# Moving key copies and block-mean writes of an attention + gated-FFN kernel from VectorE to ScalarE

## The chip, the cores and the metric

The kernel runs on one core of one Trainium2 chip. Its time is the device time of one launch in microseconds (us). Below, PE is TensorE, DVE is VectorE, ACT is ScalarE, POOL is GpSimd and SP is SyncE, as the profile names them. A median is given over several runs. A ratio is the mean time of one kernel's fast runs over the mean time of the other's fast runs of the same rounds, so it is not quite the ratio of the medians beside it; its 95% interval stands in brackets.

## The reference, cut to what matters

Sparse attention (a band of 16 tokens plus one key and one value for each block of 32 tokens), and then a gated feed-forward network (FFN) with a residual.

```python
k_sum = k.reshape(B, H, nb, block, D).max(axis=3)     # block keys: a maximum
v_sum = v.reshape(B, H, nb, block, D).mean(axis=3)    # block values: a mean
... softmax over the band |i-j| < 16 and over the blocks ...
return np.matmul(a, np.concatenate([v, v_sum], axis=2))
# then, with x the attention's output:
ffn_out = gelu(x @ w_gate) * (x @ w_val) @ w_out
return x + sigmoid(x @ w_res) * ffn_out
```

## The kernel before

The work is cut into eight units u of 384 tokens; units 2b and 2b+1 are batch b. While the FFN of unit u runs on PE, the operands of later attention steps are prepared on the other engines. An FFN step `fo` is a group of four matmuls into g, a group of four into vv, a Gelu of g on ACT, and a product on DVE:

```python
def fo_end(gvT, fo, g, vv):
    ge = work.tile([128, TU], F32, tag="ge", name="ge")
    nc.scalar.activation(ge[:], g[:, 0:TU], AF.Gelu)           # ACT, L404
    nc.vector.tensor_mul(gvT[:, fo, :], ge[:], vv[:, 0:TU])    # DVE, L405
```

g and vv take turns in a pool of four PSUM banks. In the FFN of units 3 and 5 DVE also prepares the keys and values of batches 2 and 3:

```python
def k_rest(kw):                       # L206
    ... nc.vector.tensor_max(km, ...)                           # L209
    nc.vector.tensor_reduce(out=ks, in_=km, op=ALU.max)         # L211: block keys
    nc.vector.tensor_copy(kw[:, 1:NT, 0:WIN], kw[:, 0:NT - 1, OWN + QT - WIN:OWN + QT])      # L213
    nc.vector.tensor_copy(kw[:, 0:NT - 1, POST:POST + WIN], kw[:, 1:NT, OWN:OWN + WIN])      # L214
    nc.vector.tensor_copy(kw[:, :, BLK0:BLK0 + NB], ks broadcast)                            # L215

def turn_sums():                      # a transpose on SP's DMA queue
    nc.sync.dma_start_transpose(out=vsB, in_=vsT)               # L271

def vsum_bc(b, hp, lo, hi):           # block means into vext, from vsB
    ... nc.vector.tensor_scalar_mul(dst, vsB broadcast, 1.0 / BLK)                           # L303

# in the loop over fo, units 3 and 5 (nb is the batch being prepared):
fo_step(st, gvT, fo)                                            # g, vv, Gelu, product
if fo in (1, 3):        v_spread(b, 0, HT // 2, fo // 2)        # DVE copies in vext, L291 and L294
if 5 <= fo < 9:         vsum_bc(b, fo - 5, 0, HT)
if fo == 0:             turn_sums(); turn_batch(nb, NP - 1, NP)
if fo in (0, 2, 4, 11): k_rest(kW[nb % 2][...])
```

The softmax here doesn't subtract the row's maximum and nothing guards it: scores larger than these inputs give would overflow.

## Time and profile before

| | before |
|---|---|
| time, median of 3 runs | 259.73 us (259.49 to 260.19) |
| span of the profiled run | 257.9 us |
| busy: PE / DVE / ACT / POOL | 97% / 69% / 50% / 39% |
| one FFN step on PE (two groups of 0.65 us) | 1.30 us |
| PE time lost in the FFN of unit 3 / unit 5 | 0.97 / 0.23 us |

The rows to look at are those of the instructions that will move. From the groups by line, each shape apart, of the kernel before (columns: line, engine, operation, tiles, shapes, count, busy us, mean ns of one, idle us before them):

```profile
L303 DVE TENSOR_SCALAR vext<-vsB 32x768 bf16<-32x768 bf16 x16 | 6.1, 380 | 0.5
L213 DVE COPY kW<-kW 128x176 bf16<-128x176 bf16 x12 | 3.7, 310 | 0.0
L214 DVE COPY kW<-kW 128x176 bf16<-128x176 bf16 x12 | 3.3, 279 | 0.0
```

The mean of L213 is 310 ns, although its shortest instance takes 198 ns: some instances took much longer, up to 0.59 us in unit 3. Of the L303 writes (median 360 ns) only the first of unit 3 was long, 0.66 us. Of these rows 8 of 16 and 8 of 12 will move.

### The profile page before, as it was taken

How to read it: one execution, taken by the hardware profiler on the slowest of the kernel's cores; microseconds unless marked ns; L12 is line 12 of the kernel's file. 1: busy time of each engine (PE TensorE's matmuls, PEld its weight loads, DVE VectorE, ACT ScalarE, POOL GpSimd, SP SyncE). 2: the span in 40 equal slices, each digit the busy share in tenths (PEclk: the TensorE clock that was granted, in tenths of full speed). 3: DMA queues.
4: the chain of work that ended last, by engine and by line, in shares of the span. 5: the costliest groups of instructions: out<-in, count | busy, mean ns of one | idle time of the engine just before them, and what ended most of it. 6: DMA issues, size and time to landing. Idle time of an engine off the chain costs nothing.

```text
span 257.9 us, 5755 instructions
## 1 busy us (share of the span) xinstructions
PE 250.2 (97%) x2249; PEld 139.5 (54%) x2249; DVE 178.3 (69%) x426; ACT 129.5 (50%) x223; POOL 101.0 (39%) x139
## 2 busy tenths in 40 slices
PE   7989999999999999999999999999999999999993
PEld 3546555566545555555554565555554665556543
DVE  5756866595598878679959768679768853764333
ACT  4855369455635637553373537453473537443310
POOL 7995542795699910996650100020001000010000
PEclk9999999999999999999999999999999999999999
DMA  7999999999999999999994995165003200130012
GB/s 157 151 151 193 199 202 199 142 209 123 151 152 165 179 129 167 125 186 202 154 134 90 146 145 103 31 153 68 1 3 86 84 0 0 33 137 3 1 41 83
DMA packets 117899, 30.16 MB, mean 117 GB/s; under 512 B 104816, under 2 KB 115504, under 8 KB 117872
## 3 DMA queue, kind: packets, MB, share of 16 engines
q0 software_dynamic: 86640, 19.11, 86.7%
q1 hardware_dynamic: 31232, 10.69, 25.6%
q8 instruction: 17, 0.28, 0.5%
q14 instruction: 10, 0.08, 0.1%
HBM read 32.51 MB, written 6.29 MB: 150 GB/s over the span
## 4 chain that ended last, share of the span: by engine, by line
PE 79%; DVE 7%; DMA 5%; POOL 4%; issue 2%; ACT 1%; POOLq 0%; DVEq 0%
PE f L432 22%; PE vv L398 19%; PE g L398 18%; PE r L416 8%; PE ao L362 3%; DMA k_sb<-in_k_dram 3%; PE gv L548 3%; DMA vext<-in_v_dram 2%; PE s L330 2%; DVE gvT L405 2%; PE xp L381 1%; POOL k_sb L175 1%; POOL vext L100 1%; DVE ks L211 1%; DVE vext L294 1%
## 5 line engine op out<-in xcount | busy, mean ns | idle before, releaser
L398 PE MATMUL vv<-xT,w_val 128*128 128x384 bf16 x364 | 74.5, 326 | 0.1
L404 ACT ACTIVATE ge<-g 128x384 f32<-128x384 f32 x87 | 42.7, 491 | 63.3 <-PE g L398 37.0
L398 PE MATMUL g<-xT,w_gate 128*128 128x384 bf16 x348 | 71.3, 326 | 0.4 <-DVE gvT L405 0.2
L405 DVE TENSOR_TENSOR gvT<-ge,vv 128x384 bf16<-128x384 f32 x91 | 50.0, 553 | 27.5 <-PE vv L398 25.5
L432 PE MATMUL f<-w_out,gvT 128*128 128x512 bf16 (+2 forms) x312 | 68.4, 363 | 0.0
L398 PEld LDWEIGHTS <-w_val 128*128 128x128 bf16 x368 | 36.0, 98 | 24.0 <-issue 0.4
L398 PEld LDWEIGHTS <-w_gate 128*128 128x128 bf16 x352 | 34.1, 98 | 23.2 <-issue 1.1
L432 PEld LDWEIGHTS <-gvT 128*128 128x128 bf16 x312 | 28.3, 98 | 28.2
L443 POOL DMA_DIRECT2D out_dram<-o x12 | 6.5, 544 | 90.9 <-DVE rz L370 76.0
L422 ACT ACTIVATE th<-r 128x512 f32<-128x512 f32 x24 | 14.2, 602 | 24.8 <-PE r L416 24.8
L437 DVE SCALAR_TENSOR_TENSOR th<-th,f 128x512 f32<-128x512 f32 (+2 forms) x26 | 16.7, 642 | 12.3 <-PE f L432 8.5
L175 POOL DMA_DIRECT2D k_sb<-in_k_dram x24 | 19.8, 839 | 12.5 <-DMA w_out<-in_moe_w_out_dram 5.2
L416 PE MATMUL r<-w_res,xT 128*128 128x512 bf16 x96 | 24.4, 380 | 0.0
L100 POOL DMA_DIRECT2D vext<-in_v_dram x28 | 23.2, 875 | 1.5 <-PE g L398 1.2
L175 POOL DMA_DIRECT2D q_sb<-in_q_dram x24 | 20.0, 875 | 1.6 <-DMA k_sb<-in_k_dram 1.4
L347 DVE TENSOR_TENSOR P<-P,maskt 128x768 bf16<-128x768 bf16 x28 | 15.3, 556 | 7.2 <-ACT P L336 3.9
L372 DVE TENSOR_TENSOR xn<-ao,rz 128x384 bf16<-128x384 f32 x32 | 17.8, 558 | 1.1
L383 ACT COPY xT<-xp 128x384 bf16<-128x384 bf16 x20 | 9.3, 482 | 16.5 <-PE xp L381 14.8
L439 DVE SCALAR_TENSOR_TENSOR o<-th,xn 128x512 f32<-128x512 f32 (+2 forms) x26 | 16.9, 651 | 0.9
L336 ACT ACTIVATE P<-s,bias_t 128x384 bf16<-128x384 f32 x32 | 16.8, 579 | 1.3 <-PE s L330 1.3
L339 ACT ACTIVATE P<-s,bias_t 128x768 bf16<-128x768 f32 x16 | 14.5, 904 | 3.5 <-PE s L330 3.4
L175 POOL DMA_DIRECT2D v_sb<-in_v_dram x16 | 13.2, 850 | 2.8 <-DMA q_sb<-in_q_dram 2.5
(99 smaller groups left out, 236.0 us busy)
## 6 DMA issues: line engine op xcount, KB each, us to landing
out_dram<-o POOLq DMA_DIRECT2D x12, 256.0 KB, 2.4
out_dram<-o SPq DMA_DIRECT2D x11, 256.0 KB, 4.2
vext<-in_v_dram POOLq DMA_DIRECT2D x20, 128.0 KB, 7.4
k_sb<-in_k_dram POOLq DMA_DIRECT2D x24, 96.0 KB, 7.7
q_sb<-in_q_dram POOLq DMA_DIRECT2D x24, 96.0 KB, 5.5
w_gate<-in_moe_w_gate_dram POOLq DMA_DIRECT2D x6, 256.0 KB, 8.5
w_val<-in_moe_w_val_dram POOLq DMA_DIRECT2D x6, 256.0 KB, 9.1
w_out<-in_moe_w_out_dram POOLq DMA_DIRECT2D x3, 512.0 KB, 14.9
```

The costliest lines, as they stand in the source:

```text
L100: nc.gpsimd.dma_start(out=dst, in_=v[b, :, lo:hi, :].rearrange("h p d -> p h d"))
L175: nc.gpsimd.dma_start(out=sb[b][:, h // 2, :, h % 2 * D:h % 2 * D + D], in_=src[b, h].rearrange("(c p) d -> p c d", c=NC))
L336: nc.scalar.activation(P[:, hh].rearrange("p t q -> p (t q)"), s[hh][:, 0:TU], AF.Exp, scale=scale, bias=bias_t[:])
L347: nc.vector.tensor_mul(Pf, Pf, maskt.unsqueeze(1).to_broadcast([128, 2 * HT, QT]))
L372: nc.vector.tensor_mul(xn, ao[:, :, :, 0:D], rz.to_broadcast([128, NSUB, 2, D]))
L398: nc.tensor.matmul(acc[:, 0:TU], w[:, ko, fs], st["xT"][:, ko, :], start=(ko == 0), stop=(ko == KO - 1))
L404: nc.scalar.activation(ge[:], g[:, 0:TU], AF.Gelu)
L405: nc.vector.tensor_mul(gvT[:, fo, :], ge[:], vv[:, 0:TU])
L416: nc.tensor.matmul(r[:], st["xT"][:, ko, ss], w_res[:, ko, :], start=(ko == 0), stop=(ko == KO - 1))
L432: nc.tensor.matmul(st["f", sub][:, 0:c1 - c0], gvT[:, fo, ss], w_out[:, fo, c0:c1], start=(fo == 0), stop=(fo == FO - 1))
L437: nc.vector.scalar_tensor_tensor(th, th, 1.0, f[:, 0:c1 - c0], ALU.add, ALU.mult)
L439: nc.vector.scalar_tensor_tensor(o[:, 0:c1 - c0].rearrange("p (k d) -> p k d", d=128), th.rearrange("p (k d) -> p k d", d=128), 0.5, st["x ...
```

## The change

Its intent: ACT has room in the FFN steps of units 3 and 5 (7.7 us busy of 17.1 in unit 3), DVE has little (14.7 us busy), so the two neighbor-key copies of each key step and the block-mean writes of the first half go to ACT.

```diff
-        def k_rest(kw):
+        def k_rest(kw, copy=nc.vector.tensor_copy):
...
-            nc.vector.tensor_copy(kw[:, 1:NT, 0:WIN], ...)
-            nc.vector.tensor_copy(kw[:, 0:NT - 1, POST:POST + WIN], ...)
+            copy(kw[:, 1:NT, 0:WIN], ...)
+            copy(kw[:, 0:NT - 1, POST:POST + WIN], ...)
...
-        def vsum_bc(b, hp, lo, hi):
+        def vsum_bc(b, hp, lo, hi, mul=nc.vector.tensor_scalar_mul):
...
-                nc.vector.tensor_scalar_mul(dst, ..., 1.0 / BLK)
+                mul(dst, ..., 1.0 / BLK)
...
                 if 5 <= fo < 9:
-                    vsum_bc(b, fo - 5, 0, HT)
+                    vsum_bc(b, fo - 5, 0, HT, nc.scalar.mul)
...
-                    k_rest(kW[nb % 2][(0, 2, 4, 11).index(fo)])
+                    k_rest(kW[nb % 2][(0, 2, 4, 11).index(fo)], nc.scalar.copy)
```

## The prediction

> **What bounds the kernel now.** I read the page's first part, the chain that ended last, then the chain and the timeline of the two stretches that the change touches.
>
> ```profile
> PE 250.2 (97%) x2249; PEld 139.5 (54%) x2249; DVE 178.3 (69%) x426; ACT 129.5 (50%) x223; POOL 101.0 (39%) x139
> ```
>
> TensorE (PE) is busy for 97% of the 257.9 us span, so moving work between VectorE (DVE) and ScalarE (ACT) can win only where PE waits for one of them. The chain over the whole span is PE almost throughout. The change acts in the feed-forward steps of unit 3 (112.9 to 129.6 us) and unit 5 (170.6 to 186.6 us), and there the chain leaves PE. Part of it in unit 3 (start, length, what):
>
> ```profile
> 120.44 0.46 DVE gvT L405
> ...
> 121.67 0.56 DVE gvT L405
> ...
> 122.53 0.55 DVE ks L211
> 123.08 0.07 DVE kW L213
> ...
> 123.36 0.44 DVE gvT L405
> ...
> 123.94 0.66 DVE vext L303
> 124.59 0.03 issue
> 124.62 0.56 DVE gvT L405
> ```
>
> Here DVE runs without a gap and PE waits for it. How much, the timeline tells. A step is four g and four vv matmuls, 0.65 us each group, so each group should start 0.65 us after the last:
>
> ```profile
> 120.04 0.81 PE L398 MATMUL vv<-xT,w_val 128*128 128x384 bf16 x4
> 120.96 0.81 PE L398 MATMUL g<-xT,w_gate 128*128 128x384 bf16 x4
> 122.92 0.81 PE L398 MATMUL vv<-xT,w_val 128*128 128x384 bf16 x4
> 123.96 0.81 PE L398 MATMUL g<-xT,w_gate 128*128 128x384 bf16 x4 [0.22 <-DVE gvT L405]
> 125.25 0.81 PE L398 MATMUL g<-xT,w_gate 128*128 128x384 bf16 x4
> 126.21 0.81 PE L398 MATMUL vv<-xT,w_val 128*128 128x384 bf16 x4
> ```
>
> The second of each pair is late: 120.96 against 120.69 (0.27), 123.96 against 123.57 (0.39), 126.21 against 125.90 (0.31), together **0.97 us in unit 3**. In unit 5 there is one such place: a vv group starts at 180.34 and the next g at 181.22 in place of 180.99, **0.23 us**. Both sum to 1.20 us, 0.46% of 259.73: the most that this change can give.
>
> **What the Trainium skill says.** "Perfetto Trace Analysis", section Optimizing Scalar/DVE Operations: offloading to ScalarE may make sense when DVE is saturated, though a DVE perf mode is faster for the single operation. The trace agrees on the first half: DVE is busy 5.81 of the 6.00 us from 115.0 to 121.0, ACT 2.46.
>
> "VectorE: DVE Perf Modes", section on the TRN2 errata: ScalarE needs 224 + elements cycles from SBUF to SBUF and 172 + elements from PSUM, at 1.2 GHz. The trace agrees: the 96x512 cast from SBUF took 619 ns (rule 613), the 128x384 copy from PSUM 482 ns (rule 463).
>
> "SBUF — State Buffer", section Who interferes with whom: DVE's two-port modes and GpSimd (POOL) share a port pair as an exclusive lock; ACT never waits for it. The trace agrees, as the same L213 copy shows in unit 3 beside POOL's DMA issues, and in unit 5 without them:
>
> ```profile
> 116.11 0.82 POOL L175 DMA_DIRECT2D v_sb<-in_v_dram  x1
> 116.36 0.57 DVE L213 COPY kW<-kW 128x176 bf16<-128x176 bf16 x1
> 117.78 2.46 POOL L175 DMA_DIRECT2D v_sb<-in_v_dram  x3 [0.85 <-DMA q_sb<-in_q_dram]
> 119.67 0.59 DVE L213 COPY kW<-kW 128x176 bf16<-128x176 bf16 x1
> 177.26 0.20 DVE L213 COPY kW<-kW 128x176 bf16<-128x176 bf16 x1
> ```
>
> Both long copies end with the POOL instruction (116.93 and 120.24), so a copy of 0.20 us began about 0.2 us before that: I take it that the lock comes free 0.2 us before the POOL record ends.
>
> "ScalarE: Activation LUTs", section Table sets: copy is in every set, so no table load is added. The trace agrees so far as it has copies: ACT's copies have no loads of their own. The built program adds none either.
>
> **The change part by part.** It takes from DVE in each of the two units four pairs of key copies (L213, L214: 16 in all) and four block-mean writes (L303: 8 in all) and gives them to ACT right after the Gelu of the same step. Nothing is added on PE, POOL or the DMA queues.
>
> *Cost on ACT (estimates from the errata section).* A 176-element copy: (224+176)/1.2 = 0.33 us, a pair 0.67. A 768-element write: (224+768)/1.2 = 0.83 us, against 0.36 on DVE. ACT busy: 16 x 0.33 + 8 x 0.83 = +12 us, to about 141.5. Is it in the way? A step lasts 1.30 us. With a Gelu of 0.49, a step with a pair takes 1.16 on ACT: fits. A step with a write takes 1.32: 0.02 over, four times running, so the fourth Gelu after is late by under 0.1, with semaphore gaps perhaps 0.25. What PE tolerates follows from the PSUM banks. In the built program, vv of step n mostly takes the bank of g of step n-1, so it waits for that Gelu: g(n-1) starts at t, ends at t+0.81, its Gelu ends at t+1.34, vv(n) starts at t+1.95. Slack 0.6 us: enough. At the last step the pair delays the Exp table load by 0.7 us (129.52 to 130.2), hence the two P tiles and the first tanh; the first P reader on PE starts at 134.43, and the second P mask, done at 133.25, would be done at 133.95. Hidden.
>
> *Gain on DVE.* L213 and L214 busy in the two units: unit 3 0.57+0.51, 0.59+0.53 and twice 0.20+0.20, unit 5 four times 0.40, together 4.6 us; L303 0.66+0.36+0.36+0.37 and 4 x 0.36, 3.2 us. Some overlap in the engine, so DVE busy falls by 6 to 8 us, to about 171. What counts is the wait before PE. Without the lock, the block maximum ends at 123.08 and L215 starts at 123.22, 0.14 later, because two copies stand between; with them gone it can start about 0.04 later, as ks does behind km. That is 0.10 per key step. Behind a POOL issue the gap is 0.46 and 0.48 (116.44 to 116.90, 119.75 to 120.23), but **I don't expect all of that back**: L215, which stays, is as short per element (0.22 us for 288 elements against 0.20 for 176), so it runs in the fast two-port mode too, and it will wait for the same lock.
>
> *Unit 3, walked through with the spacings of the timeline* (gvT to km 0.47, km to ks 0.39, ks 0.55, L215 to gvT 0.14, gvT to a v spread 0.57, spread to gvT 0.73):
> - gvT0 stays at 115.03. Its ks ends at 116.44; the lock is free at 116.73; L215 starts then; gvT1 116.87, spread, gvT2 118.17.
> - Its ks ends at 119.58; lock until 120.04; gvT3 at 120.18 (was 120.37), done 120.73. g6 starts at 120.77 in place of 120.69: 0.08 late (was 0.27).
> - Spread, gvT4 at 121.48, ks ends 122.89, lock free by 122.96, gvT5 at 123.10, done 123.65. g8, due at 123.37, starts at about 123.69: 0.32 late (was 0.39).
> - No block-mean writes follow, so gvT6 and gvT7 come at 123.57 and 124.04; vv9 is due after 125.6. The third wait, 0.31, is gone.
>
> Left in unit 3: 0.40 of 0.97; **gain 0.57**.
>
> *Unit 5.* POOL issues nothing in these steps, so three key steps before gvT5 give 3 x 0.10 = 0.3 us. gvT5 ends at 180.86 in place of 181.17 and g8 is due at 180.99: the whole 0.23 goes. **Gain 0.23.** The sum is 0.80 us, and behind each unit PE is the bound without a gap, so it should reach the end. Time 259.73 - 0.8 = 258.9; as the lock may let go more than I assume, I say 258.8.
>
> **The rivals.**
> 1. All waits vanish (the lock doesn't hit L215): 1.20 us, 258.5. For it: L215 is never seen long before. Against: it always stands right behind an L213 that has already waited.
> 2. ACT becomes the wait: if the strided writes took 1.2 us in place of 0.83, the Gelus would slip 0.4 us a step, 1.6 after four, over a slack of 0.6 to 1.2 us. PE would wait some 0.5 us per unit: 259.7, no gain. Against: ACT's copies with similar strides (L202 at 799 ns for 768 elements, from PSUM) keep to the rule.
> 3. The gain is hidden or lost in noise: runs before span 259.49 to 260.19. A gain given back at a DMA-fed stage after the units would make 259.7. Against: PE shows no wait there to be turned into one.
>
> **Range and chances.** Low 258.0 is the full 1.20 with the runs' scatter below it; high 259.7 is no gain. Neither rival reaches 2% (5.2 us): over 2% faster would need PE time that isn't idle, over 2% slower a stall of some 5 us on ACT, twelve times what it has now of over-full steps. So 0.01, 0.98, 0.01.
>
> **What will show each step right or wrong.** ACT rows for L213/L214 of 0.33 to 0.4 us and L303 of 0.83 to 0.9; no new table loads. DVE busy near 171, ACT near 141.5. Gaps of the g and vv starts: right if three gaps of unit 3 sum to about 0.4 us and that of unit 5 is gone; rival 1 if all are gone. A long L215 (0.4 to 0.6 us) beside a POOL issue shows that the lock wait moved. The prediction is wrong if a PE group waits for a Gelu that stands behind an ACT write, or if the chain in these units still runs along DVE with as much lost as before.

## The result, and the profile after

The changed kernel took 259.69 us (median of 6 runs, 259.30 to 260.44) against 259.58 us of the kernel before (6 runs, 258.84 to 260.19). The ratio is 1.001 [0.9986, 1.0033]. The median is just inside the range that was given, at its upper end, but the forecast gain of 0.9 us did not come.

The work moved as planned. From the page of the changed kernel, the busy line (compare the one that the prediction shows), and from its groups by line the rows of the moved instructions on ACT:

```profile
PE 249.6 (97%) x2249; PEld 139.0 (54%) x2249; DVE 172.9 (67%) x402; ACT 140.0 (54%) x247; POOL 101.0 (39%) x139
...
L303 ACT ACTIVATE vext<-vsB 32x768 bf16<-32x768 bf16 x8 | 6.8, 848 | 2.2 <-DMA vsB<-vsT 2.0
...
L214 ACT COPY kW<-kW 128x176 bf16<-128x176 bf16 x8 | 2.7, 338 | 0.0
...
L213 ACT COPY kW<-kW 128x176 bf16<-128x176 bf16 x8 | 2.6, 331 | 0.0
```

DVE fell by 5.4 us and ACT rose by 10.5 us. That DVE fell by less than the forecast 6 to 8 us goes with a rise of 1.0 us in the copy that stayed, L215 (the experiments with sums_early show why). Its row by groups, first in the kernel before, then in the changed one:

```profile
L215 DVE COPY kW<-ks 128x288 bf16<-128x288 bf16 x12 | 2.6, 218 | 0.0
...
L215 DVE COPY kW<-ks 128x288 bf16<-128x288 bf16 x12 | 3.6, 297 | 0.3
```

The instructions cost on ACT what the prediction estimated (331, 338 and 848 ns). The new thing is at the end of the row of L303: ACT stood idle 2.2 us in front of these writes, 2.0 of it for the transfer that fills vsB. What PE made of that stands in the waits of PE and of ACT in unit 3 (columns: engine, tile and line that waited, what it waited for, us in total, times, longest):

```profile
PE vv L398 <- ACT ge L404: 1.3, 1, 1.3
...
ACT vext L303 <- DMA vsB<-vsT: 2.0, 1, 2.0
```

And in order of time, the changed kernel's timeline of unit 3 around that wait (start, length, engine, line, what, and in brackets the idle time before it):

```profile
121.20 0.49 ACT L404 ACTIVATE ge<-g 128x384 f32<-128x384 f32 x1 [0.35 <-PE g L398]
121.65 0.81 PE L398 MATMUL g<-xT,w_gate 128*128 128x384 bf16 x4
122.95 0.81 PE L398 MATMUL g<-xT,w_gate 128*128 128x384 bf16 x4
123.58 0.55 DVE L405 TENSOR_TENSOR gvT<-ge,vv 128x384 bf16<-128x384 f32 x1
123.69 0.85 ACT L303 ACTIVATE vext<-vsB 32x768 bf16<-32x768 bf16 x1 [2.00 <-DMA vsB<-vsT]
124.56 0.49 ACT L404 ACTIVATE ge<-g 128x384 f32<-128x384 f32 x1
125.11 0.81 PE L398 MATMUL vv<-xT,w_val 128*128 128x384 bf16 x4 [1.34 <-ACT ge L404]
```

Read it from the bottom. The vv group of step 7 was due 0.65 us after the g group before it, at 123.60, and started at 125.11, **1.51 us late**. It needed the bank of g of step 6, which had been complete at 122.46 (121.65 + 0.81), but the Gelu that empties that bank ran only at 124.56, because ACT had an L303 write ahead of it in its queue. That write would have started at 121.69, when the Gelu of step 5 ended; it started at 123.69, when vsB had arrived.

When vsB arrives is told by the view of that tile. First the kernel before, then the changed one (count, then ns of one issue, min/median/max, and the first and last start):

```profile
L271 SPq DMA_TRANSPOSE vsB<-vsT x2: 1257/1584/1910, 115.0 to 169.4; - x2
...
DMA to landing us min/median/max: 2.5/5.1/7.7
```

```profile
L271 SPq DMA_TRANSPOSE vsB<-vsT x2: 1217/1222/1227, 115.9 to 171.0; - x2
...
DMA to landing us min/median/max: 2.5/5.1/7.6
```

There are two such transposes. The one of unit 3 is issued at 115.94 in the changed kernel and lands 7.6 us later, at 123.5. The one of unit 5 takes 2.5 us, from 170.97, and has long landed when its first write is due at 179.94. In the kernel before the transpose of unit 3 landed at 115.0 + 7.7 = 122.7, and DVE came to its first write only at 123.94, 11.05 us after unit 3 began (112.89). **DVE's place in the order had hidden the transfer.** Only a part of that is DVE being behind: in two runs below in which no gap precedes this write (keys_only, quiet_before) DVE still came to it 10.2 and 10.4 us after the unit's start, 0.6 and 1.0 us after vsB had landed, as on DVE a key step and the product of step 5 stand in front of it. ACT was free for the same write 7.84 us after the start (121.69 against 113.85), 2 us too early, and had to stand and wait, with the Gelus behind it.

The sum closes. The three gaps of unit 3 in the kernel before (0.97 us) are gone and one of 1.51 us has come; the gap of unit 5 (0.23 us) is gone and nothing has come. That is 1.51 - 1.20 = +0.31 us. The two traces agree: unit 3 starts 0.96 us later in the second (113.85 against 112.89), in code that is the same, and the last DVE instruction starts 1.27 us later (255.40 against 254.13), 0.31 us more. The spans differ by only 0.6 us, because the last transfers end sooner in the second. In time 0.31 us would be a ratio of 1.0012; the measured 1.001 is near it, but its interval is too wide to test it.

### The profile page after: what moved, and what is told of

Its sections match the earlier page's. It is cut to its first block, busy times and chain, and to the rows that moved or that the text cites. A ratio compares the mean times of both kernels' runs of the same rounds, so it can differ in the third digit from the quotient of the medians.

```text
span 258.5 us, 5769 instructions
## 1 busy us (share of the span) xinstructions
PE 249.6 (97%) x2249; PEld 139.0 (54%) x2249; DVE 172.9 (67%) x402; ACT 140.0 (54%) x247; POOL 101.0 (39%) x139
## 4 chain that ended last, share of the span: by engine, by line
PE 64%; DMA 17%; POOL 10%; DVE 5%; issue 2%; ACT 0%; DVEq 0%; POOLq 0%; ACTq 0%
PE f L432 19%; PE vv L398 16%; PE g L398 15%; PE r L416 7%; DMA w_out<-in_moe_w_out_dram 6%; DMA w_gate<-in_moe_w_gate_dram 4%; DMA qT<-q_sb 4%; DMA vext<-in_v_dram 4%; PE gv L548 3%; POOL vext L100 3%; POOL q_sb L175 2%; PE ao L362 2%; PE s L330 2%; POOL w_val L161 1%; POOL w_gate L160 1%
```

## The experiments

**Theory A**: the first block-mean write stands in ACT's queue before vsB has landed, and the Gelu behind it holds the PSUM bank that PE needs. **Rivals**: B, the gap is an accident of one execution; C, the key copies delay the Gelus; D, ACT has too much work in these steps; E, the write waits for something of the POOL queue; F, the means have to leave DVE for the gain.

Every run gave a correct result. "Gaps" are PE's delays beyond 0.65 us from one g or vv group to the next, read from the one profiled execution of each. "By gaps" is (sum of gaps - 1.20)/260 + 1, with 1.20 from the one profiled execution of the kernel before; how far its gaps vary from execution to execution was not measured.

| run | gaps of unit 3 | unit 5 | by gaps | median us | before | ratio [95%] |
|---|---|---|---|---|---|---|
| whole_again | 0.98 | 0 | 0.999 | 260.52 | 260.02 | 1.0003 [0.996, 1.0046] |
| keys_only | 0.21 | 0.28 | 0.997 | 259.63 | 260.02 | 0.9977 [0.9942, 1.0013] |
| means_only | 0.32 + 1.43 | 0.22 | 1.003 | 260.80 | 260.02 | 1.0019 [0.9982, 1.0057] |
| means_late | 0 | 0 | 0.995 | 258.86 | 260.02 | 0.9954 [0.9915, 0.9993] |
| means_late_again | 0 | 0 | 0.995 | 259.41 | 260.08 | 0.9945 [0.99, 0.999] |
| sums_early | 0.20 + 0.41 + 0.64 | 0 | 1.000 | 258.84 | 260.03 | 0.9963 [0.9931, 0.9995] |
| late_and_early | 0 | 0 | 0.995 | 258.87 | 260.08 | 0.9955 [0.9907, 1.0004] |
| keys_act_means_late_dve | 0 | 0 | 0.995 | 259.25 | 260.03 | 0.9984 [0.9945, 1.0022] |
| all_dve_means_late | 0.13 | 0.22 | 0.997 | 259.61 | 260.03 | 0.9989 [0.996, 1.0018] |
| sums_tardy | 7.01 | 0 | see there | 268.15 | 260.03 | 1.032 [1.0286, 1.0354] |
| quiet_before | 0 | 0.28 | see there | 262.48 | 260.08 | 1.0063 [1.0021, 1.0106] |
| quiet_late | 0 | 0 | see there | 261.26 | 260.08 | 1.0025 [0.9984, 1.0066] |

The runs were made in three groups, each on one chip, with 11 runs of the kernel before beside each group. The executions of one kernel spread by 1 us and more there, so most intervals are 0.3 to 0.5% wide to each side. A difference of one tenth of a per cent is therefore read from the gaps, and a time is used only to check their sum.

### The change again: whole_again

No edit.

> The changed kernel once more, as the yardstick of this group. Theory A (the first block-mean write stands on ScalarE in front of a Gelu and waits there for the transpose that fills vsB, which lands only 7.6 us after its issue): again one PE gap of about 1.5 us in unit 3 in front of a vv group, ended by the Gelu, no gaps in unit 5, and a time within 0.2% of the kernel before. Theory B (the gap was an accident of that one execution): no such gap, and the time about 1.2 us (0.5%) below the kernel before.

Again there was one gap, in front of the vv group of step 7 and ended by the Gelu, and none in unit 5. It was 0.98 us where about 1.5 was expected, but its profiled run was slow, so its size is not compared. In it ACT waited 1.5 us for vsB. Theory B falls: the gap is there each time, and the time equals that of the kernel before.

### One half of the change each: keys_only and means_only

```diff
 # keys_only, against the changed kernel
-                    vsum_bc(b, fo - 5, 0, HT, nc.scalar.mul)
+                    vsum_bc(b, fo - 5, 0, HT)
 # means_only, against the changed kernel
-                    k_rest(kW[nb % 2][(0, 2, 4, 11).index(fo)], nc.scalar.copy)
+                    k_rest(kW[nb % 2][(0, 2, 4, 11).index(fo)])
```

> Only the key copies on ScalarE; the block means are written by VectorE as before. Theory A: ScalarE never waits for vsB; the two gaps in front of g groups of unit 3 (0.27 and 0.39 us) and the one of unit 5 (0.23) go; VectorE waits for vsB near its first write, which may leave up to 0.3 us of the third gap; time 0.9 to 1.2 us below the kernel before (ratio 0.9955 to 0.9965). Rival C (ScalarE's key copies themselves delay Gelus): gaps ended by a Gelu remain in steps 0 to 5 and the time is no lower than the kernel before.

> Only the block-mean writes on ScalarE; the key copies stay on VectorE. Theory A: the first write waits for vsB, the PE gap in front of the vv group reaches the same end, so unit 3 loses about 1.5 us in all as in the whole change, and the 0.23 us gap of unit 5 stays: time 0.5 to 0.8 us above the kernel before (ratio 1.002 to 1.003). Rival C (the key copies are at fault): faster than the kernel before by 0.3 us or more, as the third gap (0.31 us) is gone.

With the keys alone the gap in front of the Gelu's bank is gone and no Gelu is late; what stays is one gap of 0.21 us and one of 0.28 us in front of vv groups, in the steps where DVE writes the means. The ratio, 0.9977, lies near the 0.997 of its gaps. This is in part a miss: 0.9 to 1.2 us was expected, no gap in unit 5, and a wait of DVE for vsB. DVE waited for nothing at its first write; vsB had landed at 123.8 (116.3 + 7.5):

```profile
124.39 0.46 DVE L303 TENSOR_SCALAR vext<-vsB 32x768 bf16<-32x768 bf16 x1
```

With the means alone the long gap is back, as the waits of PE in unit 3 show, and the old gap in front of g with it:

```profile
PE vv L398 <- ACT ge L404: 1.3, 1, 1.3
PE g L398 <- DVE gvT L405: 0.2, 1, 0.2
```

So rival C falls: the block-mean writes bring the new wait, the key copies do not. In this profile the 2.3 us for which ACT stood in front of the write are put down to a load of v_sb on the POOL queue and not to vsB, although vsB landed at 123.3 (115.44 + 7.9) and the write started at 123.44. That is rival E, and the next runs decide it.

### Give the transfer time: means_late and means_late_again

```diff
-                if 5 <= fo < 9:
-                    vsum_bc(b, fo - 5, 0, HT, nc.scalar.mul)
+                if 7 <= fo < 11:
+                    vsum_bc(b, fo - 7, 0, HT, nc.scalar.mul)
```

> The whole change, but the four block-mean writes stand in steps 7 to 10 in place of 5 to 8, 2.6 us later, when vsB has landed. Theory A: ScalarE waits for nothing there, all gaps of units 3 and 5 (1.20 us before, 1.5 after) are gone, time about 1.2 us below the kernel before (ratio 0.9955), 1.5 below the whole change. Rival D (the writes overload ScalarE, 0.85 us and a Gelu of 0.49 in a step of 1.30, whatever they wait for): the gap moves with them to steps 8 to 11 and the time stays within 0.3 us of the kernel before.

> means_late a second time, since its first interval reached from 0.9915 to 0.9993. Theory A: no or small gaps in units 3 and 5 (up to 0.4 us where a key step of VectorE meets a GpSimd issue), ratio 0.995 to 0.998. If the first result was luck, the ratio is 0.999 or more.

From the timeline of means_late, unit 3, the first write and what follows it:

```profile
123.73 0.85 ACT L303 ACTIVATE vext<-vsB 32x768 bf16<-32x768 bf16 x1
124.31 0.81 PE L398 MATMUL vv<-xT,w_val 128*128 128x384 bf16 x4
124.60 0.49 ACT L404 ACTIVATE ge<-g 128x384 f32<-128x384 f32 x1
124.96 0.81 PE L398 MATMUL g<-xT,w_gate 128*128 128x384 bf16 x4
125.11 0.84 ACT L303 ACTIVATE vext<-vsB 32x768 bf16<-32x768 bf16 x1
```

The transpose was issued at 115.4 and took 7.7 us, so vsB was there at 123.1, 0.6 us before the write was reached; no bracket stands behind the write, and the PE groups start 0.65 us apart. PE waits for nothing in unit 3. The ACT stream is just as full as in the changed kernel (write, Gelu, write, Gelu: 1.38 us a step), so rival D falls. The time is 0.9954 and 0.9945 of the kernel before in two groups on two chips, both intervals under 1: 1.2 us of 260, all that there was to win. This version beats the kernel before, and its fast runs also beat those of the changed kernel in the same group (mean 258.92 against 260.31 us of whole_again).

### Move the transfer instead: sums_early and sums_tardy

```diff
 # sums_early, against the changed kernel
+                if half == 0 and 1 < nb < B and fo == FO - 1:
+                    turn_sums()
                 if half == 1 and 1 < nb < B and fo == 0:
-                    turn_sums()
                     turn_batch(nb, NP - 1, NP)
 # sums_tardy: turn_sums() at half == 1 and fo == 3, behind turn_batch
```

> The whole change with the block-mean writes in steps 5 to 8 as changed, but the transpose that fills vsB is issued at the end of the even unit, in front of three output transfers in place of behind them. Theory A (vsB's landing is what the write waits for): it lands some 6 us sooner, before step 5, the ScalarE wait (2.0 us) and the 1.5 us PE gap are gone, time about 1.2 us below the kernel before (ratio 0.9955). Rival E (the write waits for value loads of the GpSimd queue, as one profile names them): the gap stays at 1 us or more and the time equals the kernel before within 0.3 us.

> The whole change with the transpose that fills vsB issued three steps later, behind the third key transposes and the third query transpose: about 6 us later in unit 3 (after 122 in place of 116). Theory A: the PE gap in unit 3 grows from 1.5 to between 4 and 7.5 us, with the Gelu as its end; unit 5, where the transpose lands in 2.5 us, shows 0 to 2 us; time 3 to 7 us above the kernel before (ratio 1.012 to 1.027). Rival E: the gap stays near 1.5 us.

Sent 7 us sooner (108.8), vsB is no longer waited for: ACT stands in front of no write, at the same place in its queue as in the changed kernel:

```profile
120.67 0.85 ACT L303 ACTIVATE vext<-vsB 32x768 bf16<-32x768 bf16 x1
```

Sent about 5 us later (120.83), it is waited for 7.5 us and PE stops:

```profile
129.46 0.85 ACT L303 ACTIVATE vext<-vsB 32x768 bf16<-32x768 bf16 x1 [7.50 <-DMA vsB<-vsT]
...
130.87 1.44 PE L398 MATMUL vv<-xT,w_val 128*128 128x384 bf16 x4 [6.84 <-ACT ge L404]
```

The issue moved 4.89 us (115.94 to 120.83) and the landing took 8.5 in place of 7.6 us; together that is 5.8 us, and ACT's wait grew by 5.5 us and PE's gap by 5.5 us (1.51 to 7.01). The wait follows the transpose, so it is the transpose, and rival E falls. The time was worse than expected, 1.032 in place of at most 1.027, because the granted PE clock was down to half when PE went on; the windows of the same profile show it (columns: window, its length, then busy time with count of PE, PEld, DVE, ACT and POOL, PEclk, DMA, GB/s):

```profile
130.80:133.00 2.20, 2.13 (x7) 0.99 (x7) 1.11 (x2) 2.13 (x4) 1.38 (x2) 0.50 3.17 145
133.00:135.00 2.00, 2.00 (x8) 0.90 (x7) 0.02 (x1) 1.42 (x3) 0.00 (x0) 0.50 3.88 126
135.00:137.00 2.00, 2.00 (x10) 1.02 (x9) 0.53 (x1) 0.49 (x1) 0.00 (x0) 0.65 0.16 6
137.00:140.00 3.00, 3.00 (x41) 1.79 (x40) 1.41 (x3) 1.49 (x4) 0.00 (x0) 1.00 0.00 0
```

Over the first two windows, after the stop, the granted clock was 0.50. Five groups took from 130.87 to 136.83, 5.96 us in place of 3.25: another 2.7 us. 7.01 + 2.7 - 1.2 = 8.5 us, 1.033.

In sums_early the other part of the prediction came true, the part that the changed kernel's own profile did not show in unit 3: L215 waiting for the lock between DVE and POOL. Three L215 copies took 0.48, 0.55 and 0.65 us in place of 0.22. Two of them, each behind the POOL issue that it met:

```profile
116.01 0.82 POOL L175 DMA_DIRECT2D v_sb<-in_v_dram  x1 [0.65 <-DMA q_sb<-in_q_dram]
116.38 0.48 DVE L215 COPY kW<-ks 128x288 bf16<-128x288 bf16 x1
...
119.49 0.82 POOL L175 DMA_DIRECT2D v_sb<-in_v_dram  x1 [1.66 <-DMA q_sb<-in_q_dram]
119.80 0.55 DVE L215 COPY kW<-ks 128x288 bf16<-128x288 bf16 x1
```

They end with the POOL instruction or within 0.04 us of it (116.86 against 116.83, 120.35 against 120.31). The two other DVE copies that stay, L291 and L294, took 1.02 and 1.09 us in place of 0.70 and 0.69. In that execution DVE was late again and made gaps of 0.20, 0.41 and 0.64 us in front of g groups, as many as in the kernel before. Its ratio, 0.9963 over six runs, is better than these gaps give (1.000), so most executions probably lost less; that whether L215 meets a POOL issue changes from run to run is likely, but not shown, as each kernel has one profile. In the changed kernel's profiled run it waited for none in unit 3 (0.23 us each time), but in unit 1, where nothing was moved, it did, twice (0.69 and 0.55 us, no more than 0.22 in the kernel before). The second time:

```profile
72.54 0.83 POOL L175 DMA_DIRECT2D k_sb<-in_k_dram  x1
72.66 0.20 DVE L213 COPY kW<-kW 128x176 bf16<-128x176 bf16 x1
72.77 0.20 DVE L214 COPY kW<-kW 128x176 bf16<-128x176 bf16 x1
72.88 0.55 DVE L215 COPY kW<-ks 128x288 bf16<-128x288 bf16 x1
```

### The moment or the engine: keys_act_means_late_dve, all_dve_means_late, late_and_early

```diff
 # keys_act_means_late_dve, against means_late
-                    vsum_bc(b, fo - 7, 0, HT, nc.scalar.mul)
+                    vsum_bc(b, fo - 7, 0, HT)
 # all_dve_means_late, against the kernel before: 5 <= fo < 9 and fo - 5 become 7 <= fo < 11 and fo - 7
 # late_and_early: means_late with the edit of sums_early
```

> Key copies on ScalarE, block means on VectorE but in steps 7 to 10. Theory A with the moment of the writes as what counts, not their engine: no PE gap in either unit, time as means_late, about 1.2 us below the kernel before (ratio 0.9955). Rival F (the means have to leave VectorE): gaps of 0.2 us or more in front of g or vv groups remain, as in keys_only (0.21 and 0.28), only later.

> The kernel before with nothing moved to ScalarE, the block-mean writes in steps 7 to 10. What the move of the keys alone is worth in gaps: the two gaps in front of g groups of unit 3 (0.27 and 0.39 us) and that of unit 5 (0.23) should stay, as the key copies make them; the third of unit 3 (0.31) should go; time 0.3 us below the kernel before (ratio 0.999). If instead all gaps go, the key copies were no cause, and means_late owes nothing to ScalarE.

> means_late and sums_early together: nothing that ScalarE waits for can be late. As sums_early had no ScalarE wait left and means_late neither, nothing more can come of it: ratio as means_late, 0.995 to 0.998. If it is lower by 0.3% or more, a wait was left that the profiles did not show.

With the keys on ACT and the means late but on DVE there is no gap in either unit, so rival F falls: for the means it is the moment that counts. Its time (0.9984, up to 1.0022) neither confirms nor denies the 1.2 us. With everything on DVE and the means late, the third gap of unit 3 is gone as expected, the gap of unit 5 stays (0.22), and of the two in front of g groups only one of 0.13 us showed where 0.27 and 0.39 were expected: a partial miss, in the steps where copies can wait for POOL: here L213 took 0.38 us at the first key step and 0.20 at the next two. With gaps of 0.35 us against 0 and ratios of 0.9989 and 0.9984, these runs do not settle how much of the 1.2 us is owed to the keys on ACT and how much to the later writes. The two edits together do no better than either: nothing was left to wait for.

### The lock by itself: quiet_before and quiet_late

```diff
 # against the kernel before (quiet_before) and against means_late (quiet_late)
-            if u == 3:
-                for c in range(NC + 1):
-                    load_values(3, c)
...
-                    load_rows(3)
+                    load_rows(3, 0, 2)                   # keys and queries only
+                if u == 3 and fo == FO - 1:
+                    gate(gvT[0:1, fo, 0:1])
+                    load_rows(3, 2, 3)                   # the values
+                    for c in range(NC + 1):
+                        load_values(3, c)
```

> The kernel before, all on VectorE, but the GpSimd queue issues the value loads of batch 3 at the end of the feed-forward steps of unit 3 in place of among them. Lock theory (a VectorE copy waits for the port pair while GpSimd writes descriptors): no L213, L214, L215 or L303 of unit 3 is longer than 0.37 us, the steps run at the spacing of unit 5 (1.69 and 1.31 us), so the gaps of unit 3 fall from 0.97 to under 0.2 us and that of unit 5 (0.23) stays; time 0.7 to 1.0 us below the kernel before (ratio 0.996 to 0.9975). Rival G (VectorE's instruction count alone makes the gaps): unit 3 keeps 0.6 us or more.

> means_late with the same quiet GpSimd queue. Lock theory: no gap in either unit in any run, so 1.2 us below the kernel before (ratio 0.9955), and no better than 0.2 to 0.3 us below quiet_before, which then shows how little the move to ScalarE is worth once the lock is out of the way. If the loads come too late in their new place, a wait for them shows in unit 4 and the time is above means_late.

In unit 3 this did what the lock theory says. With the value loads out of these steps, all key copies on DVE take their short time and no copy or block-mean write is long, from the timeline of quiet_before:

```profile
116.23 0.20 DVE L213 COPY kW<-kW 128x176 bf16<-128x176 bf16 x1
116.34 0.20 DVE L214 COPY kW<-kW 128x176 bf16<-128x176 bf16 x1
116.46 0.22 DVE L215 COPY kW<-ks 128x288 bf16<-128x288 bf16 x1
...
144.99 0.32 PE L545 MATMUL gv<-xT,w_gate 128*128 128x384 bf16 x1 [2.19 <-DMA xT<-xn]
```

The gaps of unit 3 fall from 0.97 to 0 with every instruction still on DVE; rival G falls, as far as one execution each can tell: without the waits for the lock DVE is early enough with all its instructions. The time nevertheless rose, to 1.0063, where at most 0.9975 was expected. The last line says why: the loads now stand beside the transposes of xT at the turn to unit 4, PE waits 2.19 us for one of them (it did not wait there in the kernel before), and the clock falls once more (0.62 and 0.53 in the next two windows of 2 us). quiet_late, expected at 0.9955 and measured at 1.0025, has the same wait, 1.54 us, and no fall of the clock. So the place chosen for the loads was bad and these two are no faster kernels; whether a good place exists was not tried.

## Why the prediction was wrong, point by point

- **What bounds the kernel, and the most that can be won**: right. 1.20 us of PE gaps was the whole prize; means_late has no gap and gained 0.46% and 0.55% (intervals of 0.4% and more to each side).
- **Cost of the moved instructions on ACT**: right (0.33 and 0.83 us estimated, 0.331 to 0.338 and 0.848 measured). A step with a write took 1.38 us on ACT in place of 1.32. No table load came.
- **The gaps of DVE**: 0.57 us of unit 3's 0.97 was to come back, as L215 would take over the wait for the lock. In the profiled run it waited for no POOL issue in unit 3 and the whole 0.97 came back (rival 1); in sums_early it waited three times and nothing did. The mechanism stands, the size was a guess at a coincidence. The argument against rival 1, that L215 "always stands right behind an L213 that has already waited", was a misreading: in unit 5 of the same profile L213 takes 0.20 us, so there it had not waited. The gap of unit 5 went as forecast.
- **The step that failed** is the sentence on ACT: a step with a write "takes 1.32: 0.02 over", and with "Slack 0.6 us: enough". The slack was right: the Gelu of step 6, unhindered, would have ended at 122.99 (122.46 + 0.04 + 0.49), 0.61 us before vv was due at 123.60. What was put against it was only the time that the write takes, not the time at which it can start. The write needs vsB, which the prediction never mentions. In its profile DVE shows no wait for it, and its issue at 115.0 looks early. In its place the runs showed ACT standing 2.0 us in front of the write; past the slack, that is a gap of 1.51 us in unit 3, which cancelled the 1.20 us won.
- **Rival 2** named ACT as the new wait, but by the length of the writes. They were as short as estimated. The closing sentence did name the sign, a PE group that waits for a Gelu behind an ACT write, and that is what came.
- **Behind the units** nothing was lost: from the end of unit 3 to the start of unit 5 both profiles take 41.13 us (129.46 to 170.59, and 130.95 to 172.08).

## What to carry to other kernels

Before work goes to an idle engine, look up when each of its inputs arrives, not only whether the old engine waited for it: an engine that comes to the work late, because it is behind or because other work stands in front, hides the latency of a transfer, and an engine that comes to it sooner exposes it. An engine that works through its queue in order makes everything behind the waiting instruction late, here a Gelu that held a PSUM bank. So put moved work where its input has landed, or send the input sooner; two FFN steps of delay turned a change worth nothing into the full gain.

## What the Trainium skill lacked or had wrong

- "DMA: Bandwidth & Descriptors" gives a fixed cost for a transfer and rates for the transpose in DMA, but no time to landing for a small transpose beside other traffic. In the changed kernel the same transpose of four 128-column blocks landed after 2.5 us in unit 5 and after 7.6 us in unit 3; during the two the core's DMA moved 157 and 194 GB/s, so the rate alone does not explain the difference, and its cause was not tested. Sent later (sums_tardy) it took 4.4 and 8.5 us.
- "SBUF — State Buffer", section Who interferes with whom, says that the loser of the shared port pair is blocked until the other instruction ends. The runs agree in kind. They add that a DVE copy blocked by a POOL issue of 0.82 us ends within 0.06 us of that record's end (116.86 against 116.83, 73.43 against 73.37), so with its own 0.2 us it starts before the record ends, and that not the whole record blocks: two copies ran at 0.20 us inside the record from 72.54 to 73.37, and the third, at 72.88, was held.
- "TensorE: Matmul & The Clock Gate", section What's actually happening, puts the fall to half clock after an idle window of about 3.4 us. Here a wait of 2.19 us was already followed by a granted clock of 0.62 and 0.53 over the next 4 us, while waits of 1.34 and 1.54 us were not. In sums_tardy PE stopped at 124.02 and the clock was 1.00 to 126.0, 0.94 to 126.2 and 0.50 from there: it fell about 2.2 us into the stop.
- "Perfetto Trace Analysis", section Optimizing Scalar/DVE Operations, says that moving work to ACT may make sense when DVE is saturated. It does not say that the work then meets its inputs sooner; here that cost 2.0 us of ACT's time and 1.51 us of PE's.
